# A fused transformer block on one core: how the first weights and tokens are loaded, and the order of the first microseconds

## The chip, the core and the metric

The kernel runs on one core of one Trainium2 chip. A core has a matmul engine (TensorE, PE in the profile, with its weight loads as PEld), VectorE (DVE), ScalarE (ACT), GpSimd (POOL) and SyncE (SP), which here only issues DMA transfers. Each engine works through its own list of instructions in order and waits on semaphores for the others. The metric is the device time of one execution in microseconds; lower is better.

## The reference

Input x is 2048 tokens of 448 values (D), in bf16. The block is an adaLN transformer layer:

```
mod = silu(c) @ w_mod                      # six rows of 448: sa, ca, ga, sb, cb, gb
h = layernorm(x) * (1 + ca) + sa
x = x + ga * A(h)                          # A: attention
h = layernorm(x) * (1 + cb) + sb
x = x + gb * B(h)                          # B: layernorm, 448->1792, gelu, 1792->448
```

A has 16 heads of 28 values. Each token sees 8 keys: itself and every second token before it, 14 back at the most. q, k and v come from one matrix wqkv (448 rows of 3 · 448).

## The kernel before

**Tiles.** Tokens are handled as even and odd streams (NS = 2), so that a window of 8 keys two apart becomes 8 neighbours in one stream. A tile p (0 to 7) holds 128 partitions with two tokens each: a row of x_all for one tile is two tokens of 448 bf16 values, 1792 bytes. The 448 input values of a matmul are three blocks of 128 rows and a rest of 64 rows; the rest rows are held twice, in the upper and the lower 64 partitions, so that two half-height matmuls can run for two outputs.

**The start.** Tile 0 and then tile 1 go through: statistics and normalization on VectorE (`stats` L455, `normalize` L477), transposes on TensorE into PSUM (`tr`, L532), scale and shift by the modulation into hT (`affine` L494), and the Q and K projections into qT and kT (`front_qk` L580). Tiles 2 to 7 go in pairs: their normalized rows are transposed by DMA (zT, L527), then `affine`, then the projection with the weights as moving operand (`natural_qk`, L614), whose result is again transposed by DMA into kT and qT (L631). Attention runs in 9 batches; the three matmuls of a batch's scores, sums and outputs are the lines L738, L760 and L771. V is made in L706 and L695, the output projection in L803, the two layers of B in L548 (through `summed`) and L883.

**The modulation.** c is turned into a column of PSUM by four matmuls (`c_cols`). silu is c / (1 + exp(−c)): exp on ScalarE, two operations on VectorE that leave the reciprocal in e_c, a product into silu_bf (128 × 4), and a ScalarE copy that repeats each of its columns 32 times into silu_bc. Then `mod_cols` makes the rows sa and ca as columns: matmuls over wm_st (three blocks of w_mod) and over wm_r (the rest).

**The staged weights of Q and K.** wqk_st holds three blocks of 128 rows with the Q and K columns of wqkv, wqr_st the 64 rest rows twice. In the projection of tiles 0 and 1 each head takes 32 columns of the array: `spread` (L432) copies from wqk_st into Wqk with a step of 28 columns and runs of 32, so that each head's run reaches four columns into the next head. The last head's run reaches four columns past the end of K, and this is why the loads take 900 columns instead of 896.

**Loads.** `load` (L317) puts transfers on SP's list. In the order of the list before: x tile 0, w_mod blocks, two halves of the w_mod rest, x tile 1, Q, K block 0, the two rest loads, blocks 1 and 2, x tiles 2 and 3 in one, x tiles 6 and 7, V's blocks, one V rest, x tiles 4 and 5, and so on.

**What sets the order.** Every step is a task, made by `add` with its engine, and the program order is a list written out by hand: ORDER names tasks by number, with a letter where a task goes to another than its first engine; SLOTS gives each buffer its place in its room (P is PSUM). `emit` walks through both. An entry such as `55+12@55` puts twelve filler matmuls over zeros ahead of task 55 on TensorE. The durations in the calls of `add` are estimates that are not used when the list is there. What an engine does next is thus fixed, and only semaphores decide when.

Of the kernel before, what the change touches and what calls it, by code (L numbers as in the profile page):

```python
# [49 lines left out]
]  # L50
ORDER = """
3 14 17 0 1 15 5 9 10 18 11 16 13 19 20 2 6 24 21 73 55+12@55 26 12 71 25 56 72 74 57 75 22 58 77 23 59 60 27 62 61 76
32 4 67 66 68+11@68 78 63 28 108 64 30 110 69 79 84:A 89:P 31 65 70 109 111 80 88:P 83 34 81 112:P 87:A 29 101+9@101
85 90:A 93:P 36 114 94+3@94 82 95 113 102 92:A 91 115:D 86 103 116 96 120:A 144 97 99 104 106 117:A 135 98 118:A 142
105 119:A 145 143 133 100 146 121 136 134 126 137 148 107 147 149:D 7 138 127 150 122 124 139 129 190 123 198 191 140
200 128 141 125 199 269 271 130 236 270 40 207 33 209 38 201 241 208 210 237 211 185 35 39 242 202 8 187 151:A 238 154
239 153 152 186 212 159 203 213 188 204 214:D 155 240 215 278 205 279 280 156 160 206 307:R 281 161 243 282 272 192
273:A 37 157 189 171 162 308:D 194 172 283 193 244 218 173 163 219 195 275 158 284 196 216 167 217 285 246 447:P 197
286 164 168 165 228 169:D 174 274 309 276:D 312 277 220 313 310 314 166 221 229 225 230 224 311 170 222:D 247 315 245
176 317 316 175 226 248 233 232 318 227 290 249 289:A 319 287:A 43 234 223 288 320 250 558:P 46 45 559 321 47 231 253  # L60
345 342 346 251 560 303 482:P 252 44 324 343 322 291 254 561 323 325 347 326 344 292 304 255 327 293 348 328 373:R 256
305 329 294 257 350 258 375 378 52 330 376 340:R 53 333 235 379 377 334 331 374 296 300 332 41 295 259 351 49 335 380
299 336 341 337 260 297 382 262 381 263 301 261 349 264 338:A 352 483 383 339 384 265 484 266 449 353 267 485 385 268
# [3 lines left out]
487 401 490 454 403 402 436 453 455 370 444 404 434 371:D 456 372 491 457 488 405 459 493 458 460 445 492 435 494 461  # L67
# [3 lines left out]
513 515:D 547 599 516 564 602 481 568 569 570 604 571 603 546 605 572 548 606 573 628 607 608 574 549 635 575 550 609  # L71
612 636 577 630 578 637 610 629 576 640 579 638 581 639 611 613 580 582 583 641 631 586 633 587 651 584 614 632 585
616 588 615 617 642 618 648 646 647 621 654 634 619 645 622 652 620 656 649 623 644 658 643 625 624 650 589 590 626
591:A 664 655 627 653 439 657 592 659 556 665 662 663 674 666 660 661 669 667 675 668 678 676 679 677 686 672 673 671
687 681 670 680 690 691 694 697 693 682 688 692 685 695 683 689 701 684 698 696 709 699 710 702 711 712 705 700 703
706 704 707 708
# [77 lines left out]
def kernel(  # L154
# [68 lines left out]
    silu_bf = cst.tile([128, KT], BF16, name="silu_bf")  # L223
# [739 lines left out]
```

## Time and profile before

| | |
|---|---|
| median of 3 runs | 168.64 us (167.93 to 169.38) |
| the profiled execution | 169.75 us, its span 168.1 us |
| busy | TensorE 96%, VectorE 69%, ScalarE 61%, GpSimd 28% |
| granted clock of TensorE | full, over the whole span |
| DMA | 18.78 MB in 35574 packets, mean 112 GB/s |

A line of the page or of an answer from the trace names engine, line of the kernel, operation, the tile written and the tiles read, the shape and the number of instructions. In a timeline the first two numbers are the start (microseconds from the start of the span) and the length; brackets give how long the engine was idle before it and which engine or transfer ended that. A letter q behind an engine (SPq) is its sequencer, which issues transfers. The span runs from the first to the last instruction; the execution's own time has 1.65 us beside it.

### The profile page before, as it was taken

Reading aid. Unit: us, or ns where it says so; the run is one execution under the profiler, and the core shown is the slowest. Engines: PE = TensorE matmul, PEld = TensorE weight load, DVE = VectorE, ACT = ScalarE, POOL = GpSimd, SP = SyncE. Lnnn points to the kernel's source line nnn. Section 1 sums busy time; section 2 is a strip of 40 time slices with the busy share of each in tenths; the row PEclk is TensorE's granted clock in tenths of the full one; section 3 lists DMA queues with packets and bytes.
Section 4 is the critical chain, followed back from the end, with each engine's and each line's share of the span. In section 5 each row is a group of like instructions: output and inputs, shape, how many; then the busy total and the mean of one; then the engine's idle time right before and its main releaser. Section 6 shows DMA issues by size and latency. Waiting matters only on the chain.

```text
span 168.1 us, 4962 instructions
## 1 busy us (share of the span) xinstructions
PE 161.5 (96%) x2126; PEld 83.4 (50%) x2126; DVE 115.8 (69%) x271; ACT 102.7 (61%) x142; POOL 47.7 (28%) x76
## 2 busy tenths in 40 slices
PE   7989989999997999999999999999999999999992
PEld 4768544345544544435565444556434455444562
DVE  6869899879899689998738877474798930400032
ACT  3368987779489954759866376956627730097300
POOL 4135252300361201269300113820003870007200
PEclk9999999999999999999999999999999999999999
DMA  5999989799997999910091000008110027110003
GB/s 153 325 335 297 168 265 134 152 201 170 221 200 182 236 150 236 169 35 0 4 139 46 4 0 0 4 0 97 35 55 0 0 43 195 49 60 0 0 0 109
DMA packets 35574, 18.78 MB, mean 112 GB/s; under 512 B 28508, under 2 KB 34593, under 8 KB 35553
## 3 DMA queue, kind: packets, MB, share of 16 engines
q1 hardware_dynamic: 35548, 18.47, 53.0%
q8 instruction: 16, 0.26, 0.7%
q14 instruction: 6, 0.04, 0.1%
q10 hardware_dynamic: 4, 0.00, 0.0%
HBM read 9.81 MB, written 1.84 MB: 69 GB/s over the span
## 4 chain that ended last, share of the span: by engine, by line
PE 81%; DMA 10%; DVE 2%; POOL 2%; issue 1%; SPq 1%; ACT 1%; POOLq 0%; DVEq 0%
PE p L883 26%; PE p L548 22%; PE pw L803 7%; PE pq L548 6%; PE p L554 4%; DMA x_all<-in_A_x_dram 4%; PE po L771 3%; PE lt L738 3%; PE pv L706 3%; PE pv L548 3%; DMA wm_st<-in_w_mod_dram 3%; DMA zT<-zy 2%; DMA kT<-zy 2%; PE pq L554 1%; PE pd L760 1%
## 5 line engine op out<-in xcount | busy, mean ns | idle before, releaser
L864 ACT ACTIVATE hm<-p,b_col 128x512 bf16<-128x512 f32 x56 | 33.9, 692 | 29.9 <-PE p L554 27.3
L883 PE MATMUL p<-w_s,hm 128*128 128x448 bf16 (+1 forms) x238 | 44.1, 342 | 0.0
L548 PE MATMUL p<-yT,w_s 128*128 128x512 bf16 x168 | 38.1, 379 | 0.0
L469 POOL TENSOR_TENSOR rs_all<-mvs,neg_half 128x2 f32<-128x2 f32 x22 | 16.7, 766 | 57.9 <-DVE mvs L458 57.8
L883 PEld LDWEIGHTS <-hm 128*128 128x128 bf16 x238 | 22.7, 98 | 19.2 <-issue 0.8
L889 DVE TENSOR_TENSOR x_all<-p,x1p 128x896 bf16<-128x896 f32 (+2 forms) x10 | 8.9, 902 | 25.9 <-PE p L883 25.9
L548 PEld LDWEIGHTS <-w_s 128*128 128x128 bf16 x168 | 15.8, 98 | 20.9 <-issue 2.9
L456 DVE BATCH_NORM_STATS2 stt<-x_all 128x6 f32<-128x448 bf16 x32 | 18.7, 610 | 1.2 <-DMA x_all<-in_A_x_dram 1.0
L745 ACT ACTIVATE et<-lt 128x928 bf16<-128x928 f32 x18 | 16.1, 947 | 5.3 <-PE lt L738 5.1
L841 POOL TENSOR_TENSOR x1p<-x_all,gbb_bc 128x448 f32<-128x448 bf16 x16 | 17.8, 1134 | 0.0
L548 PE MATMUL pq<-wqk_st,hT 128*128 128x448 bf16 x72 | 15.2, 354 | 0.6 <-DVE hT L502 0.5
L788 DVE TENSOR_TENSOR qT<-po,den 128x912 bf16<-128x912 f32 x9 | 9.9, 1104 | 7.0 <-ACT den L782 5.6
L751 DVE TENSOR_TENSOR et<-et,mask 128x928 bf16<-128x928 bf16 x18 | 11.6, 672 | 2.4 <-ACT et L745 2.4
L803 PE MATMUL pw<-wo_s,qT 128*128 128x448 bf16 x64 | 13.2, 353 | 0.0
L780 ACT ACTIVATE den<-pd 128x928 f32<-128x928 f32 x9 | 8.5, 940 | 5.8 <-PE pd L760 5.7
L819 DVE TENSOR_TENSOR h<-h,mod_bc 128x896 bf16<-128x896 bf16 x16 | 11.1, 709 | 0.3
L548 PEld LDWEIGHTS <-hT 128*128 128x128 bf16 x72 | 6.4, 98 | 7.7 <-issue 1.3
L628 ACT CAST zy<-pq 128x896 bf16<-128x896 f32 x10 | 9.0, 906 | 2.0 <-PE pq L554 1.9
L810 DVE TENSOR_TENSOR x_all<-pw,x_all 128x896 bf16<-128x896 f32 x8 | 8.7, 1088 | 1.7 <-PE pw L803 1.5
L782 ACT ACTIVATE den<-den,den_bias 128x928 f32<-128x928 f32 x9 | 9.6, 1072 | 0.2
L478 DVE TENSOR_SCALAR zy<-h,mvs,rs_all 128x448 bf16<-128x448 bf16 x16 | 6.6, 456 | 4.4 <-POOL rs_all L469 4.3
L456 DVE BATCH_NORM_STATS2 stt<-h 128x6 f32<-128x448 bf16 x16 | 9.4, 613 | 0.2
(115 smaller groups left out, 183.4 us busy)
## 6 DMA issues: line engine op xcount, KB each, us to landing
w_s<-in_B_w_dram SPq DMA_DIRECT2D x7, 224.0 KB, 4.2
out_dram<-x_all SPq DMA_DIRECT2D x7, 224.0 KB, 2.2
x_all<-in_A_x_dram SPq DMA_DIRECT2D x3, 448.0 KB, 6.0
wmod<-in_w_mod_dram SPq DMA_DIRECT2D x3, 448.0 KB, 7.0
w_s<-in_B_w_dram SPq DMA_DIRECT2D x3, 448.0 KB
wqk_st<-in_A_wqkv_dram SPq DMA_DIRECT2D x3, 225.0 KB
wm_st<-in_w_mod_dram SPq DMA_DIRECT2D x1, 672.0 KB
x_all<-in_A_x_dram SPq DMA_DIRECT2D x2, 224.0 KB, 2.6
```

The costliest lines, as they stand in the source:

```text
L456: add("DVE", 0.53, lambda: nc.vector.bn_stats(out=stt[:, w, b, 0:6], in_=src()), reads=reads, bufs=bufs, after=early if w == b == 0 else ( ...
L469: ways = {"POOL": (0.55 + 0.17 * n, lambda: nc.gpsimd.tensor_tensor(out=r, in0=v, in1=neg_half[:, 0:n], op=ALU.pow))}
L548: nc.tensor.matmul(out(), lhsT=lhs(kt, slice(0, 128)), rhs=rhs(kt, slice(0, 128)), start=first and kt == 0, stop=not first and kt == KT - 2)
L745: exps.append(add("ACT", 0.83, lambda half=half, lt=lt: nc.scalar.activation(out=et.t[:, 2 * half:2 * half + 2].rearrange("p r m c -> p r ...
L751: nc.vector.tensor_tensor(out=ev, in0=ev, in1=mask[:], op=ALU.mult)
L782: exps.append(add("ACT", 0.96, lambda: nc.scalar.activation(out=den.t[:], in_=den.t[:], func=ACT.Exp, scale=-1.0, bias=den_bias[:]), bufs= ...
L788: nc.vector.tensor_tensor(out=qT[:, :, LEAD + q00:LEAD + q00 + 2 * WQ], in0=po.t[:, :, 0:NS * 4 * WQ].rearrange("p j (m c) -> p m j c", c=WQ),
L803: nc.tensor.matmul(pw.t[:, s, 0:D], lhsT=qT[:, KT * s + ft, LEAD + 128 * p:LEAD + 128 * p + 128], rhs=wo_s[:, ft, :], start=(ft == 0), sto ...
L819: add("DVE", 0.55, lambda vec=vec, op=op: nc.vector.tensor_tensor(out=h2.t[:], in0=h2.t[:], in1=vec.unsqueeze(1).to_broadcast([128, NS, D] ...
L841: add("POOL", 1.0, lambda n=n: nc.gpsimd.tensor_tensor(out=x1p.t[:, n, :], in0=xn(p, n), in1=gbb2_bc[:], op=ALU.add), reads=[f"x{p}", "gbb ...
L864: gelus.append(add("ACT", 0.585, lambda f=f, a=a, p1=p1s[g]: nc.scalar.activation(out=hm.t[:, f].rearrange("p n c -> p (n c)"), in_=p1.t[: ...
L883: nc.tensor.matmul(p2.t[:, n, 0:c1 - c0], lhsT=hm.t[:, f, n, q * 128:(q + 1) * 128], rhs=w2_s[:, f, c0:c1], start=(f == parts[0][0]), stop ...
```

## The change

Five edits, all at the start of the program, with the order list and the buffer list made anew:

- wqk_st and wqr_st become 928 columns wide. The loads bring 896 columns, and two memsets on VectorE, beside that of neg_half, set the four columns behind them to zero. The copies of `spread` wait for them.
- The two halves of each rest (of w_mod, of Q and K, of V) come in one load of 128 partitions, whose source has a leading dimension of 2: step 0 where the same rows are wanted twice, step D for w_mod.
- x tiles 2 and 3 are two loads.
- silu's product and its repetition are one VectorE operation, which writes silu_bc from e_c, read with step 0, and PSUM. The ScalarE copy is gone, and so is silu_bf.
- The two memsets of one_cb move from between tile 0's two statistics to ahead of that operation.

Tasks are numbered anew (three fewer), so nearly every number in ORDER differs. With the numbers put back, each engine's list differs in these places only:

| engine | before | after |
|---|---|---|
| SP | ... x1, QK block 0, rest, rest, block 1, block 2, x2 and x3, x6 and x7, V, V rest, x4 and x5, ... | ... x1, QK block 0, block 1, rest, block 2, x2, x3, x6 and x7, V, x4 and x5, ... (V rest whole, behind the first block of the later w_mod load) |
| TensorE | 12 fillers, c, 11 fillers, modulation rest, blocks, last column; 9 fillers, projection of tile 0 (one piece), 3 fillers, four pieces, tile 1's transposes, the third Q piece, the half-row pieces, ... | 8 fillers, c, 10 fillers, modulation blocks, last column, rest; 9 fillers, five pieces, the third Q piece, the half-row pieces, tile 1's transposes, ... |
| VectorE | one copy of `spread`, tile 1's two normalizations, copy, tail, copy | three copies, two normalizations, tail |
| ScalarE | the silu_bc copy | gone |

The buffer list gives two of the first PSUM tiles each other's places and moves one zy tile; what follows is the old sharing with other numbers.

The diff without the two lists:

```diff
-    wqk_st = sb("hm", [128, KT - 1, 2 * D + HP - DH], BF16, "wqk_st")
-    wqr_st = sb("h2", [128, 2 * D + HP - DH], BF16, "wqr_st")
+    wqk_st = sb("hm", [128, KT - 1, 2 * D + HP], BF16, "wqk_st")
+    wqr_st = sb("h2", [128, 2 * D + HP], BF16, "wqr_st")
...
-    dconst(0.06, lambda: nc.vector.memset(neg_half[:], -0.5), ["neg_half"])
+    def make_half():
+        nc.vector.memset(neg_half[:], -0.5)
+        nc.vector.memset(wqk_st.t[:, :, 2 * D:2 * D + HP - DH], 0.0)
+        nc.vector.memset(wqr_st.t[:, 2 * D:2 * D + HP - DH], 0.0)
+
+    dconst(0.2, make_half, ["neg_half", "wqpad"], [wqk_st, wqr_st])
...
-        load(lambda: nc.sync.dma_start(out=wqk_st.t[:, kt, :], in_=A_wqkv[kt * 128:kt * 128 + 128, 0:2 * D + HP - DH]), 0.62, [f"wqk{kt}"],
+        load(lambda: nc.sync.dma_start(out=wqk_st.t[:, kt, 0:2 * D], in_=A_wqkv[kt * 128:kt * 128 + 128, 0:2 * D]), 0.62, [f"wqk{kt}"],
...
-    def load_rest(a):
-        load(lambda a=a: nc.sync.dma_start(out=wqr_st.t[KS * a:KS * a + KS, :], in_=A_wqkv[(KT - 1) * 128:D, 0:2 * D + HP - DH]),
-             0.5, [f"wr{a}"], bufs=[wqr_st])
+    def both(src, n):
+
+        return bass.AP(src.tensor, src.offset, [[n, 2], *src.ap])
+
+    def load_rest():
+        load(lambda: nc.sync.dma_start(out=wqr_st.t[:, 0:2 * D], in_=both(A_wqkv[(KT - 1) * 128:D, 0:2 * D], 0)),
+             0.5, ["wr0", "wr1"], bufs=[wqr_st])
...
-        for a in range(2):
-            load(lambda a=a: nc.sync.dma_start(out=Wv[KS * a:KS * a + KS, KT - 1, :], in_=A_wqkv[(KT - 1) * 128:D, 2 * D:3 * D]),
-                 0.2, [f"wvr{a}"])
+        load(lambda: nc.sync.dma_start(out=Wv[:, KT - 1, :], in_=both(A_wqkv[(KT - 1) * 128:D, 2 * D:3 * D], 0)), 0.3, ["wvr0", "wvr1"])
...
-    for v in range(2):
-        load(lambda v=v: nc.sync.dma_start(out=wm_r.t[KS * v:KS * v + KS, :], in_=w_mod[(KT - 1) * 128:D, v * D:v * D + D]),
-             0.25, [f"wmr{v}"], bufs=[wm_r])
+    load(lambda: nc.sync.dma_start(out=wm_r.t[:], in_=both(w_mod[(KT - 1) * 128:D, 0:D], D)), 0.4, ["wmr0", "wmr1"], bufs=[wm_r])
...
-    load_rest(0)
-    load_rest(1)
-    load_x(2, 4)
+    load_rest()
+    load_x(2, 3)
+    load_x(3, 4)
...
-    add("DVE", 0.08, lambda: nc.vector.tensor_tensor(out=silu_bf[:], in0=e_c[:], in1=psc.t[:, 0, 0:128 * KT:128], op=ALU.mult),
-        reads=["e_c"], bufs=[psc], writes=["silu"], name="silu")
-    add("ACT", 0.18, lambda: nc.scalar.copy(out=silu_bc[:], in_=silu_bf[:].unsqueeze(2).to_broadcast([128, KT, HP])),
-        reads=["silu"], writes=["silu_bc"], name="silu_bc")
+    add("DVE", 0.2, lambda: nc.vector.tensor_tensor(
+        out=silu_bc[:], in0=e_c[:].unsqueeze(2).to_broadcast([128, KT, HP]),
+        in1=psc.t[:, 0, :].rearrange("p (k n) -> p k n", n=128)[:, :, 0:HP], op=ALU.mult),
+        reads=["e_c"], bufs=[psc], writes=["silu_bc"], name="silu_bc")
```

More of the change, by code (lines that the diff above doesn't have):

```diff
@@ L43 @@
 SLOTS = [
[6 rows of a table removed]
[6 rows of a table added]
 ]
 ORDER = """
[L52 to L60, printed above, removed]
@@ L72 @@
[L72 to L76, printed above, removed]
+3 14 17 0 1 15 5 9 10 18 11 16 13 19 2 6 70 53+8@53 23 20 21 54 24 68 22 69 71 55 56 72 12 25 57 74 26 59 60+10@60 58
@@ new lines @@
+73 30 61 4 64 63 75 65 27 66 105 76 29 107 81:A 86:P 32 62 67 106 108 77 80 28 78 84:A 85:P 98+9@98 87:A 91 109:P 82
+88 92 34 79 83 99 90:P 89:A 100 111 93 110 94 96 112:D 101 141 103 113 132 95 117:A 139 102 114:A 142 140 130 115:A
+143 133 116:A 131 134 145 97 118 144 146:D 7 135 147 123 136 104 195 124 119 197 121 126 137 187 138 196 266 120 188
+268 125 267 122 204 38 233 206 31 127 198 36 205 207 208 33 238 234 37 199 182 8 239 148:A 151 184 235 150 149 236 209
+156 200 210 183 201 211:D 152 237 212 185 275 202 276 277 153 157 203 304:R 278 158 240 279 269 189 270:A 35 154 186
@@ new lines @@
+168 159 305:D 191 169 280 190 241 215 170 160 216 192 272 155 281 193 213 164 214 282 243 444:P 194 283 161 165 162
+225 166:D 171 271 306 273:D 309 274 217 310 307 311 163 218 226 222 227 221 308 167 219:D 244 312 242 173 314 313 172
+245 223 230 229 315 224 287 246 286:A 316 284:A 41 231 220 285 317 247 555:P 44 43 556 318 45 228 250 342 339 343 248
+557 300 479:P 249 42 321 340 319 288 558 251 320 322 344 323 341 289 301 252 324 290 345 325 370:R 253 302 326 291 254
+347 255 372 375 50 327 373 337:R 51 330 232 376 374 331 328 293 371 297 39 329 292 256 348 47 332 377 296 333 338 334
@@ new lines @@
+257 294 379 259 378 260 298 258 346 261 335:A 349 480 380 336 381 262 481 263 446 350 264 482 382 265 445 351 303 590
[3 rows of a table added]
+400 399 433 450 452 367 441 401 431 368:D 453 369 488 454 485 402 456 490 455 457 442 489 432 491 458 492 434 514 459
+435 493 591 460 494 461 533 495 463 534 522 464 536 462 498 592 465 521 535 499 496 593 466 497 500 501 502 515 503
+524 467 526 468 525 504 469 523 470 528 507 516 505 527 519 472 517 506 473 508 471 520 537 539 518 548 509 529 474
+532 541 530 550 531 476 511 554 475 562 597 477 559 540 563 549 598 538 594 560 551 564 595 542 552 510 512:D 544 596
@@ new lines @@
+513 561 599 478 565 566 567 601 568 600 543 602 569 545 603 570 625 604 605 571 546 632 572 547 606 609 633 574 627
+575 634 607 626 573 637 576 635 578 636 608 610 577 579 580 638 628 583 630 648 584 581 611 629 582 613 585 612 614
+639 615 645 643 644 618 651 631 616 642 619 649 617 653 646 620 641 655 640 622 621 647 586 587 623 588:A 661 652 624
+650 436 654 589 656 553 662 659 660 671 663 657 658 666 664 672 665 675 673 676 674 683 669 670 668 684 678 667 677
+687 688 691 694 690 679 685 689 682 692 680 686 698 681 695 693 706 696 707 699 708 709 702 697 700 703 701 704 705
@@ L222 @@
     e_c = cst.tile([128, KT], FP32, name="e_c")
-    silu_bf = cst.tile([128, KT], BF16, name="silu_bf")
     silu_bc = cst.tile([128, KT, HP], BF16, name="silu_bc")
@@ L244, with dconst @@
     early = []
-    def dconst(us, fn, writes):
-        early.append(add("DVE", us, fn, writes=writes, after=[one], name="const " + writes[0]))
+    def dconst(us, fn, writes, bufs=()):
+        early.append(add("DVE", us, fn, writes=writes, bufs=bufs, after=[one], name="const " + writes[0]))
     def const(us, fn, writes, reads=()):
@@ L317, in load @@
     def load(fn, us, writes, bufs=(), reads=(), fills=()):
-        queue.append(add("SP", 0.5, fn, reads=reads, writes=writes, bufs=bufs, fills=fills, after=queue[-1:] if len(queue) < 4 else queue[3:4], xfer=us,
+        queue.append(add("SP", 0.5, fn, reads=reads, writes=writes, bufs=bufs, fills=fills, after=queue[-1:] if len(queue) < 3 else queue[2:3], xfer=us,
                          name="load " + writes[0]))
@@ L438, in spread @@
             dst, src = (lambda k0=k0, n=n: Wqk[:, k0:k0 + n, half]), (lambda k0=k0, n=n: heads(wqk_st.t[:, k0:k0 + n, half * D:half * D + D], H))
-            add("DVE", 0.06 + 0.18 * n, lambda dst=dst, src=src: nc.vector.tensor_copy(out=dst(), in_=src()), reads=[f"wqk{k}" for k in ks],
+            add("DVE", 0.06 + 0.18 * n, lambda dst=dst, src=src: nc.vector.tensor_copy(out=dst(), in_=src()), reads=["wqpad"] + [f"wqk{k}" for k in ks],
                 bufs=[wqk_st], writes=[f"W{half}{k}" for k in ks], port=True, name="spread",
@@ L446, in spread @@
             src = lambda rows=rows, c0=c0: heads(wqr_st.t[rows, c0:c0 + D // 2], H // 2)
-            add("DVE", 0.22, lambda rows=rows, src=src: nc.vector.tensor_copy(out=Wqr[rows, half], in_=src()), reads=[f"wr{a}"],
+            add("DVE", 0.22, lambda rows=rows, src=src: nc.vector.tensor_copy(out=Wqr[rows, half], in_=src()), reads=["wqpad", f"wr{a}"],
                 bufs=[wqr_st], writes=[f"Wr{half}{a}"], port=True, name="spread r",
@@ L455, in stats @@
     def stats(src, w, b, reads, bufs=()):
-        add("DVE", 0.53, lambda: nc.vector.bn_stats(out=stt[:, w, b, 0:6], in_=src()), reads=reads, bufs=bufs, after=early if w == b == 0 else (),
+        add("DVE", 0.53, lambda: nc.vector.bn_stats(out=stt[:, w, b, 0:6], in_=src()), reads=reads, bufs=bufs,
             writes=[f"st{w}_{b}"], name="stats")
```

5 lines of the change are left out of this document (removed), and 21 rows, old and new, of tables (ORDER, SLOTS).

## Prediction

> **What bounds the kernel now.** I read the page first, then the chain of waits in order of time, then TensorE's own waits, and then the first 23 us engine by engine. The page, section 1 and the engine line of section 4:
>
> ```profile
> span 168.1 us, 4962 instructions
> ...
> PE 161.5 (96%) x2126; PEld 83.4 (50%) x2126; DVE 115.8 (69%) x271; ACT 102.7 (61%) x142; POOL 47.7 (28%) x76
> ...
> PE 81%; DMA 10%; DVE 2%; POOL 2%; issue 1%; SPq 1%; ACT 1%; POOLq 0%; DVEq 0%
> ```
>
> TensorE is busy 96% of the span and carries 81% of the chain, so the question is where it is not. The answer on what TensorE waited for has five lines:
>
> ```profile
> PE ps_c L382 <- DVE warm_w L242: 1.3, 1, 1.3
> PE lt L738 <- issue: 0.8, 1, 0.8
> PE pq L548 <- DVE hT L502: 0.5, 1, 0.5
> PE pq L562 <- DVE Wqk L439: 0.4, 1, 0.4
> PE lt L738 <- DMA kT<-zy: 0.4, 1, 0.4
> ```
>
> The first is the start of the program. The others are single gaps of 0.4 to 0.85 us. That is all that a change at the start can collect, apart from the filler matmuls of the first 10 us, which stand in TensorE's busy time without being work. The pieces of the chain (start, length, what) show which gap belongs to what:
>
> ```profile
> 1.26 4.57 DMA wm_st<-in_w_mod_dram
> ...
> 5.85 0.43 SPq L325
> ...
> 6.32 6.00 DMA x_all<-in_A_x_dram
> ...
> 12.34 1.68 DVE stt L456 x3
> ...
> 17.56 3.38 DMA zT<-zy
> ...
> 21.04 1.71 DVE hT L502 x3
> ...
> 22.79 2.25 PE pq L548 x11
> ...
> 33.71 0.70 PE lt L738 x62
> ...
> 51.05 0.85 issue
> ```
>
> So up to 22.79 us the end is set by one thread: the load of x tiles 2 and 3 (6.32 to 12.32), their statistics, their transposes through the DMA, their affine step on VectorE, and the Q projection of tiles 2 and 3, for which TensorE waits 0.54 us. After it TensorE runs almost without a pause. Busy time by stretch (columns: PE, PEld, DVE, ACT, POOL busy, clock, DMA share, GB/s):
>
> ```profile
> 3.50:5.50 2.00, 2.00 (x12) 1.09 (x11) 1.72 (x8) 0.50 (x3) 0.00 (x0) 1.00 1.05 391
> 6.00:8.50 2.50, 2.41 (x48) 1.89 (x47) 2.40 (x15) 0.92 (x2) 0.61 (x1) 1.00 1.02 293
> 9.50:11.50 2.00, 1.57 (x17) 1.19 (x15) 1.61 (x6) 1.33 (x3) 0.79 (x2) 1.00 0.97 341
> 13.97:22.25 8.28, 8.24 (x194) 5.17 (x192) 7.27 (x25) 7.31 (x9) 4.69 (x11) 1.00 0.92 215
> 22.79:165.08 142.29, 141.03 (x1814) 69.29 (x1814) 96.71 (x193) 87.78 (x119) 38.73 (x47) 1.00 0.49 89
> ```
>
> Two second threads matter. From 13.97 to 22.25 TensorE is busy 8.24 of 8.28 us: whatever lets this block start earlier or later moves its end by as much, and only the 0.54 us behind it hides a delay. And the DMA engines are full (share 0.97 to 1.05) from 3.5 us on, but not at one rate: 391 GB/s while 1792-byte rows of w_mod are moved, 293 while the 1800-byte Q, K rows are, 341 after them.
>
> **The change, part by part.** In the order list, after its numbers are shifted for the joined tasks, each engine's order differs only in the first 16 us or so; the buffer numbers are, but for the first few PSUM tiles and two zy tiles, a renaming. From tile 1's projection on (`front_qk`, L580) the program is the old one. So the sum is made at 22.79 us and carried from there.
>
> *Rows of 1792 instead of 1800 bytes.* The staged rows are 3·128 + 2·64 = 512, that is 922 KB. At 293 GB/s they take 3.15 us; at 341, as what follows them, 2.70; at 391, as w_mod's rows of just the new length, 2.36. The gain for everything queued behind is 0 to 0.79 us. I take 0.45 to 0.79, since the low rate coincides with these rows and both neighbours have rows of 1792 bytes; 0 stays as a bound, because I see only a coincidence of rate and rows. [...]
>
> *Tiles 2 and 3 in two loads.* They do not help by themselves: VectorE's list begins these statistics with a half of tile 3 before and after the change, so it waits for the later load. Its place in the queue has the same bytes ahead. The third Q, K issue stands at 5.85, directly behind w_mod's landing (1.26 + 4.57 = 5.83); with fewer transfers ahead I expect tile 3's load to be the one that waits there, 0.47 us before the 6.32 of today's joined load. With the DMA engines full that is worth nothing. Net: tile 3 lands 0.45 to 0.79 us earlier, at 11.5 to 11.9.
>
> *What stands between it and TensorE.* VectorE must be free when it lands:
>
> ```profile
> 9.93 0.86 DVE L478 TENSOR_SCALAR zy<-x_all,mvs,rs_all 128x448 bf16<-128x448 bf16 x2 [0.18 <-POOL rs_all L469]
> 10.71 0.28 DVE L439 COPY Wqk<-wqk_st 128x512 bf16<-128x512 bf16 x1
> 10.91 0.18 DVE L491 COPY zy<-zy 128x128 bf16<-128x128 bf16 x1
> 11.02 0.28 DVE L439 COPY Wqk<-wqk_st 128x512 bf16<-128x512 bf16 x1
> ```
>
> It has finished by 11.30 today; the same operations are only reordered (both copies ahead of the two normalizations), so it is free at about 11.3 or before. The thread from 12.34 to 22.75 (statistics, GpSimd, transposes, affine) is unchanged and moves as one. Alone this would put tile 2's projection at 22.0 to 22.3.
>
> *The silu columns.* The two steps between e_c and silu_bc today:
>
> ```profile
> 5.38 0.20 ACT L467 ACTIVATE rs_all<-rs_all 128x2 f32<-128x2 f32 x1
> 6.19 0.30 ACT L398 COPY silu_bc<-silu_bf 128x128 bf16<-128x128 bf16 x1 [0.61 <-DVE silu_bf L396]
> ...
> 5.69 0.40 DVE L478 TENSOR_SCALAR zy<-x_all,mvs,rs_all 128x448 bf16<-128x448 bf16 x1 [0.33 <-ACT rs_all L467]
> 6.00 0.15 DVE L396 TENSOR_TENSOR silu_bf<-e_c,ps_c 128x4 bf16<-128x4 f32 x1
> 6.07 0.25 DVE L418 COPY wm_d<-wm_st 128x384 bf16<-128x384 bf16 x1
> ```
>
> The joined operation writes 128 values to each partition: above the 0.15 us for 4, below the 0.40 for 448, so about 0.25. It falls into the 0.33 us that VectorE idles before the normalization at 5.69. silu_bc would then be there by some 5.7 instead of 6.49. w_mod lands at 5.83, so the modulation matmuls could start 0.6 us earlier, but VectorE, which needs their result only after its statistics of tile 1, does not pass that on. What VectorE does gain is the 0.15 us of the removed operation's place and a little from the one_cb memsets that go into the idle time: 0.15 to 0.2 us for the affine steps of tile 0.
> *The added memsets and the joined rest loads.* One row for each:
>
> ```profile
> 1.28 0.06 DVE L270 MEMSET neg_half<- 128x4 f32 x1
> ...
> 1.73 1.20 SPq L349 DMA_DIRECT2D wm_r<-in_w_mod_dram  x2
> ```
>
> Two memsets of that size, 0.12 us, end within the wait for tile 0's rows. Three joins take three issues of 0.6 us off SP, one of them far behind, and the split adds one; with the DMA engines full that is zero, and if the engines ran dry it would bring the later transfers forward by up to 0.6 us. Eight fewer fillers are not work.
>
> *Tile 1's transposes behind tile 0's projection.* This costs. TensorE's list today and ScalarE's beside it:
>
> ```profile
> 11.05 0.39 PE L562 MATMUL pq<-hT,Wqk 128*128 128x256 bf16 x2 [0.43 <-DVE Wqk L439]
> 11.28 0.61 PE L535 MATMUL ptr<-ident,zy 128*128 128x128 bf16 x8
> 11.72 0.38 PE L562 MATMUL pq<-hT,Wqk 128*128 128x256 bf16 x2
> 12.04 0.61 PE L554 MATMUL pq<-hT,Wqr 64*128 64x256 bf16 x8
> ...
> 9.98 0.56 ACT L504 ACTIVATE hT<-ptr,mod_col 128x256 bf16<-128x256 bf16 x1
> 10.44 0.39 ACT L449 COPY Wqr<-wqr_st 64x256 bf16<-64x256 bf16 x1
> 11.93 0.57 ACT L504 ACTIVATE hT<-ptr,mod_col 128x256 bf16<-128x256 bf16 x1 [1.10 <-PE ptr L535]
> ```
>
> The pair at 11.05 no longer waits for a copy (it comes before the normalizations) but for ScalarE's affine step, which ends at 10.54, less 0.17: TensorE starts at 10.4. Then 0.23 for the pair, 0.32 for the next pair and the switch to half rows, 0.54 for the eight half-row matmuls: the transposes start at about 11.5, 0.2 us later than today. ScalarE's four affine steps of tile 1 follow at 12.1 to 14.05. The block at 13.97 has 0.11 us to spare against them (1.93 us of steps from 11.93), so it starts 0.1 us late and ends at 22.35.
>
> *Sum.* The projection of tiles 2 and 3 starts at the later of 22.35 (TensorE) and 22.0 to 22.3 (its data): 22.35 instead of 22.79, a gain of 0.44 us. Behind it ScalarE, SP and VectorE hang on the same two threads, so I carry it whole; the gap before the scores at 33.7 us (0.4) and the one that waited for "issue" at 51.05 (0.85) I leave. The profiled execution took 169.75 us, 168.1 of span and 1.65 around it; it would be 169.3. The median of the runs is 1.11 us lower, so 168.64 − 0.44 = **168.2 us**.
>
> **Rivals.** First, *the rows are not slower for their length*: the 293 GB/s is a disturbance of the memory, and tile 3 lands at 12.3 as today. For it: 341 GB/s afterwards is not 391 either, with rows of 1792 bytes. Then the projection starts at 22.79 as before, TensorE idles where the fillers were, and the time is 168.6. [...]
>
> Second, on the other side, *VectorE stuck behind the third weight transfer*. Its two copies of the third row block now stand ahead of tile 1's normalizations. If that block lands after 10.4 us, the copies, 0.78 us of normalizations and the 0.18 us copy end after 11.9, the transposes start 0.65 us late, and the block behind reaches 22.79 too late; landing at 10.7, the latest today's copy allows, gives 23.2, so 0.4 us slower: 169.0. Against it: both earlier blocks and the half rows go ahead as today, and any gain in rate brings it forward.
>
> Third, *more than the sum*: the later gaps (0.4 at 33.7, 0.85 at 51.05) do not come again with other timing, and tile 1 is not held up: 0.44 + 0.1 + 0.4 + 0.85 = 1.8 us, 166.8. For it: neither gap is a steady cost of a repeated instruction; against it: nothing there is changed.
>
> **How the numbers follow.** Forecast 0.5, first rival 0.27, second 0.12, third 0.11. The runs of the kernel before spread by 0.7 us to either side, so 1% (1.7 us) is about what can be told from no change. The range runs from the third rival to the second with part of that spread on top: 166.8 to 169.4. Forecast and first rival are "within 1%" whole, the second nearly, the third by half: faster 0.08, same 0.86, slower 0.06.
>
> **What would show it.** Right: over 340 GB/s between 6 and 8.5 us; VectorE's statistics of tile 3 at 11.5 to 11.9; the transposes of tile 1 behind the half-row matmuls at about 11.5 and a new TensorE gap of about 0.7 us before 14; no gap at 22.3. Wrong: DMA at 293 GB/s and statistics at 12.3 (first rival); the copies of Wqk waiting for the DMA past 10.4 (second). The sum is also wrong if the projection does start earlier and the scores at 33.7 wait longer for kT by the same amount. A TensorE that stays on its slower pace beyond 9 us, having fewer fillers, would show as longer matmuls in the first projection.

## The result, and the profile after

The changed kernel is slower, where no measurable change was forecast: 176.67 us median of 6 runs (175.95 to 177.89) against 169.02 us of the kernel before beside it (6 runs, 167.93 to 169.68). The ratio is 1.046, with an interval of 1.041 to 1.051. That is 7.6 us; the forecast was 168.2 us, with a range up to 169.4. The profiled execution took 176.53 us, 174.8 of it span, against 169.75 and 168.1. Here and below, medians and ranges hold all runs, and ratios leave out the few that lie over 1.5% above the fastest of their kernel.

The page of the changed kernel: span, busy time, the granted clock in 40 slices, the chain's shares.

```profile
span 174.8 us, 4947 instructions
...
PE 163.4 (93%) x2118; PEld 84.3 (48%) x2118; DVE 116.1 (66%) x273; ACT 102.3 (59%) x141; POOL 47.1 (27%) x76
...
PEclk9968799999999999999999999999999999999999
...
PE 81%; DMA 9%; ACT 3%; DVE 2%; SPq 2%; issue 1%; DVEq 0%
```

TensorE is busy about as long as before (163.4 us against 161.5), in a span that is 6.7 us longer: it stands still more. And its clock, full over the whole span before, now dips in slices 3 to 5, which are 8.7 to 21.9 us. What TensorE waited for (in all, times, longest, in us):

```profile
PE pq L565 <- ACT Wqk L444: 3.6, 1, 3.6
PE ps_col L413 <- DMA wm_r<-in_w_mod_dram: 1.5, 1, 1.5
PE ps_c L385 <- DVE warm_w L240: 1.3, 1, 1.3
...
```

The first two lines are new, and both lead to joined rest loads: wm_r itself, and a copy (L444) that stands on ScalarE behind a copy of the rest of Q and K. The chain shows this in a row (start, length, what):

```profile
3.88 11.68 DMA wqr_st<-in_A_wqkv_dram
...
15.58 0.40 ACT Wqr L452
15.98 0.53 ACT Wqk L444
...
16.56 1.47 PE pq L565 x6
18.03 0.97 PE pq L557 x8
19.00 0.80 PE ptr L538 x8
...
19.82 1.94 ACT hT L507 x4
```

One load of 229 KB needs 11.68 us to land, while the DMA engines move more than that in each microsecond. The stretches show what happens meanwhile, first after, then before (busy PE, PEld, DVE, ACT, POOL, granted clock, DMA share, GB/s):

```profile
10.00:15.00 5.00, 2.96 (x15) 1.87 (x13) 1.05 (x6) 0.56 (x1) 0.00 (x0) 0.74 0.99 278
15.00:20.00 5.00, 3.44 (x26) 2.17 (x27) 3.46 (x11) 1.86 (x5) 1.61 (x3) 0.66 0.44 141
```

```profile
10.00:15.00 5.00, 4.57 (x49) 3.54 (x48) 3.94 (x13) 3.90 (x9) 0.95 (x2) 1.00 1.05 372
15.00:20.00 5.00, 5.00 (x110) 3.14 (x109) 4.83 (x15) 4.11 (x5) 2.14 (x8) 1.00 0.88 168
```

All engines run dry between 10 and 15 us; DMA alone stays busy, at 278 instead of 372 GB/s. The clock of 0.74 and 0.66 is a mean: in shorter stretches it is half behind each of the two waits, and nearly full between them.

```profile
9.40:11.00 1.60, 1.21 (x6) 0.84 (x6) 1.50 (x8) 0.89 (x2) 0.43 (x1) 0.50 0.96 302
...
12.90:16.50 3.60, 0.06 (x1) 0.00 (x0) 0.51 (x2) 0.92 (x3) 0.74 (x2) 0.94 0.81 256
16.50:18.00 1.50, 1.44 (x8) 0.73 (x10) 0.95 (x3) 0.76 (x3) 0.87 (x2) 0.50 0.13 49
```

TensorE's timeline after, from the end of its wait to the Q projection of tiles 2 and 3 (L551, the last line but one) and the piece behind that (L557):

```profile
16.56 1.47 PE L565 MATMUL pq<-hT,Wqk 128*128 128x256 bf16 x6 [3.60 <-ACT Wqk L444]
17.96 1.04 PE L557 MATMUL pq<-hT,Wqr 64*128 64x256 bf16 x8
18.93 0.86 PE L538 MATMUL ptr<-ident,zy 128*128 128x128 bf16 x8
...
29.63 2.44 PE L551 MATMUL pq<-wqk_st,hT 128*128 128x448 bf16 x12
32.01 0.55 PE L557 MATMUL pq<-wqr_st,hT 64*128 64x448 bf16 x4
```

Before, one matmul of this projection ran early and the other eleven from 22.79 us, so the start of the piece behind it is the fair comparison:

```profile
21.89 0.36 PE L548 MATMUL pq<-wqk_st,hT 128*128 128x448 bf16 x1
...
24.98 0.55 PE L554 MATMUL pq<-wqr_st,hT 64*128 64x448 bf16 x4
```

32.01 − 24.98 = 7.03 us, and the span is 6.7 us longer: the whole loss lies ahead of this point.

Why one load lags is seen in the trace's completion events. An ordinary load here has sixteen completion reports, as many as the page counts DMA engines. (The two loads of c, one row each, have two, before and after.) These are the times of all reports, in us, of some loads of the changed kernel (a pair far behind the rest is set apart):

```
load                      issued   reports
rest of w_mod, joined     1.72     2.80 |                     7.84  8.05
x tile 1                           fourteen, 5.88 to  6.75 |  8.39  8.49
Q, K block 0                       fourteen, 6.58 to  7.47 |  9.01  9.08
Q, K block 1                       fourteen, 7.25 to  8.04 |  9.56  9.66
rest of Q, K, joined      3.88     4.87 |                    15.31 15.55
Q, K block 2              4.48     fourteen, 8.11 to  8.77 | 15.86 15.88
x tile 2                           fourteen, 8.80 to  9.33 | 16.41 16.47
x tile 3                           fourteen, 9.48 to 10.28 | 16.99 17.01
```

A joined load has one report 1.0 us after its issue and then only two late ones; the others have sixteen. In the kernel before, each half rest has sixteen, from 7.43 to 9.05 us. From the two late reports I infer that a joined load is carried by two engines, 64 rows each. Those two then fall behind in everything that follows: fourteen sixteenths of x tile 3 were there at 10.28 us, before the 12.3 of the old kernel, and two sixteenths came at 17.0. VectorE's last copies out of block 2 waited for all sixteen: they began at 15.91, behind the report at 15.88. Why it is two, no run shows. In the trace's record of the issues, each of these joined loads has destination sizes of 1 and 128, and each half in the kernel before 64 and 1.

### The profile page after: what moved, and what is told of

Its sections match the earlier page's. It is cut to its first block, busy times and chain, and to the rows that moved or that the text cites. A ratio compares the mean times of both kernels' runs of the same rounds, so it can differ in the third digit from the quotient of the medians.

```text
span 174.8 us, 4947 instructions
## 1 busy us (share of the span) xinstructions
PE 163.4 (93%) x2118; PEld 84.3 (48%) x2118; DVE 116.1 (66%) x273; ACT 102.3 (59%) x141; POOL 47.1 (27%) x76
## 4 chain that ended last, share of the span: by engine, by line
PE 81%; DMA 9%; ACT 3%; DVE 2%; SPq 2%; issue 1%; DVEq 0%
PE p L886 25%; PE p L551 21%; PE pw L806 7%; DMA wqr_st<-in_A_wqkv_dram 7%; PE pq L551 6%; PE p L557 4%; PE pv L709 4%; PE lt L741 3%; PE po L774 3%; DMA zT<-zy 3%; PE pv L551 3%; PE pq L557 2%; PE pd L763 1%; ACT hT L507 1%; PE pq L565 1%
## 5 line engine op out<-in xcount | busy, mean ns | idle before, releaser
L551 PE MATMUL p<-yT,w_s 128*128 128x512 bf16 x168 | 38.1, 379 | 0.0
L551 PEld LDWEIGHTS <-w_s 128*128 128x128 bf16 x168 | 15.9, 98 | 20.9 <-issue 2.9
L551 PE MATMUL pq<-wqk_st,hT 128*128 128x448 bf16 x72 | 15.0, 353 | 0.1
L551 PEld LDWEIGHTS <-hT 128*128 128x128 bf16 x72 | 6.5, 98 | 7.0 <-issue 1.2
```

Of the source, the lines that this page charges most:

```text
L551: nc.tensor.matmul(out(), lhsT=lhs(kt, slice(0, 128)), rhs=rhs(kt, slice(0, 128)), start=first and kt == 0, stop=not first and kt == KT - 2)
```

## The experiments

Two theories stood at the outset: the leading dimension of 2 puts a load on two engines, against the length of the single load, the order of the queue, or another of the five edits. Times are medians, with the kernel before timed beside each kernel; a ratio's interval is 95%. Four kernels were run once (the Q, K join alone, the two patterns without a join, the other source). A single time stands against the spread of the kernel before, 167.9 to 170.8 us in 23 runs, so it carries a conclusion only where the difference is well over that.

**The joins undone.** The changed kernel, with its order and all its other edits, but each joined load issued as two (shown for Q and K; V and w_mod likewise):

```diff
+    def halves(dst, src):
+        for a in range(2):
+            nc.sync.dma_start(out=dst(a), in_=src(a))
...
-        load(lambda: nc.sync.dma_start(out=wqr_st.t[:, 0:2 * D], in_=both(A_wqkv[(KT - 1) * 128:D, 0:2 * D], 0)),
+        load(lambda: halves(lambda a: wqr_st.t[KS * a:KS * a + KS, 0:2 * D], lambda a: A_wqkv[(KT - 1) * 128:D, 0:2 * D]),
```

> The changed kernel with its three joined loads (rest of w_mod, of Q and K, of V) each issued as two loads of 64 partitions again; order lists, row length, tiles 2 and 3 apart and the silu operation as changed. Theory (two engines): a load whose source has a leading dimension of 2 is carried out by two of the sixteen DMA engines, and these two then hold up a sixteenth share each of every later load. Then all of the loss is in the joins: the rest of Q and K lands by about 9 us instead of 15.6, and the time goes from 176.7 to within 1% of the kernel before, 168 to 169.5. Rival (order): the loss comes from the new order (rests behind block 1, transposes of tile 1 behind the half-row matmuls) or from fewer fillers and the lower clock they leave: then it stays above 174.

Measured: 169.36 us (12 runs, 168.28 to 171.87) against 168.96; ratio 1.003 (0.9995 to 1.006). The whole loss is in the joins; the rest of the change moves the time by no more than the interval, which holds 1. That is the same measured result as the forecast for the whole change, but not by its sum, as the next section shows.

**One join alone, Q and K.** The kernel before, with only this load joined:

```diff
-        load(lambda a=a: nc.sync.dma_start(out=wqr_st.t[KS * a:KS * a + KS, :], in_=A_wqkv[(KT - 1) * 128:D, 0:2 * D + HP - DH]),
...
+            src = A_wqkv[(KT - 1) * 128:D, 0:2 * D + HP - DH]
+            if a:
+                nc.sync.dma_start(out=wqr_st.t[:], in_=bass.AP(src.tensor, src.offset, [[0, 2], *src.ap]))
```

> The kernel before with one edit: the two rest loads of Q and K are one load of 128 partitions whose source has a leading dimension of 2 with step 0. Theory (two engines): each of two engines gets 64 rows of 75 to 100 ns, 5 to 6 us more work than today, so the rest lands at 12 to 14 us instead of 8.7, the later weight and token loads land 4 to 6 us late, and the time is 172 to 175. Rival (order): no order is changed, so 168 to 169.5.

Measured: 173.69 us (one run) against 168.96, so about 4.7 us, inside the 172 to 175 of the theory. (The 75 to 100 ns of a row there are packet times in the trace of before: the middle half of its 512 packets of 1800 bytes took 75 to 100 ns.) The load needed 9.19 us to land, and its copy stood on GpSimd, with the half-row part of tile 0's projection behind it (GpSimd's timeline):

```profile
13.38 0.40 POOL L455 COPY Wqr<-wqr_st 64x256 bf16<-64x256 bf16 x1 [5.54 <-DMA wqr_st<-in_A_wqkv_dram]
```

**One join alone, w_mod.** Likewise, with a step of 448 (D) instead of 0:

```diff
+                nc.sync.dma_start(out=wm_r.t[:], in_=bass.AP(src.tensor, src.offset, [[D, 2], *src.ap]))
```

> The kernel before with one edit: the two halves of the w_mod rest come in one load with a leading dimension of 2 (step 448 values, no row read twice). Theory (two engines): 64 rows of 41 ns on each of two engines, 2.3 us more than its share of 8 rows; it lands at about 8 us instead of 6.2, the modulation and everything that the two engines carry later is late by about as much, and the time is 170 to 171.5. Rival (only re-reading the same rows, step 0, is slow): 168.5 to 169.5.

Measured: 170.59 us (4 runs, 170.26 to 171.54) against 168.25; ratio 1.014 (1.009 to 1.020), so 2.3 us. What TensorE waited for, and a stretch of its windows:

```profile
PE ps_col L415 <- DMA wm_r<-in_w_mod_dram: 2.6, 1, 2.6
```

```profile
9.50:11.50 2.00, 2.00 (x36) 1.80 (x33) 1.79 (x7) 0.94 (x2) 1.01 (x2) 0.50 0.92 263
```

TensorE waits 2.6 us, until the load lands at about 9.1 (8 was expected), with two late reports, 8.70 and 9.09 us, and right behind that runs at half its clock. Step 0 is not needed for the loss: 448 does it too. (The 41 ns of a row in the theory are the median of the 896-byte packets in the trace of before.)

**One join alone, V.** The kernel of the first experiment, with V's rest joined as in the change:

```diff
-        load(lambda: halves(lambda a: Wv[KS * a:KS * a + KS, KT - 1, :], lambda a: A_wqkv[(KT - 1) * 128:D, 2 * D:3 * D]), 0.3, ["wvr0", "wvr1"])
+        load(lambda: nc.sync.dma_start(out=Wv[:, KT - 1, :], in_=both(A_wqkv[(KT - 1) * 128:D, 2 * D:3 * D], 0)), 0.3, ["wvr0", "wvr1"])
```

> The changed kernel with the joined loads of the w_mod rest and of the Q, K rest undone and that of the V rest kept. Theory (two engines): it lands some 2.3 us later and delays a sixteenth of each transfer behind it on two engines, but V's first matmuls come at 18 us and the later weights are wanted after 26 us, so no cost: 168.5 to 169.8. If it does cost, above 170.5.

Measured: 169.74 us (10 runs, 168.48 to 172.75); ratio to the kernel before 1.003 (0.999 to 1.007), as without this join. So a two-engine load that nobody wants soon costs nothing that these runs can tell. The two that are wanted soon add up to 4.7 + 2.3 = 7.0 of the 7.6 us, where the 4.7 comes from a single run. Engines can also fall behind without a join: in this kernel's profile, fourteen reports of w_mod's blocks had come by 5.75 us and two came at 7.04 and 7.07, long before V's rest was issued at 10.82. Why is open.

**The leading dimension, without a join.** Joining changes three things at once: the pattern, the size of the load and the number of issues. So two kernels keep both half loads at their size and place and change the pattern alone. The first reads its 64 rows as 2 times 32 neighbouring rows:

```diff
-        load(lambda a=a: nc.sync.dma_start(out=wqr_st.t[KS * a:KS * a + KS, :], in_=A_wqkv[(KT - 1) * 128:D, 0:2 * D + HP - DH]),
...
+            (pitch, n), cols = src.ap
+            nc.sync.dma_start(out=wqr_st.t[KS * a:KS * a + KS, :], in_=bass.AP(src.tensor, src.offset, [[pitch * n // 2, 2], [pitch, n // 2], cols]))
```

> The kernel before with one edit: its two rest loads of Q and K stay two loads of 64 partitions with the same rows and bytes, but the source is written with a leading dimension of 2 (2 times 32 rows). Theory (two engines, set by the leading dimension): both loads go to the same two engines, 64 rows each, so the delays are those of the joined load: rest at 12 to 14 us, 172 to 175 in all. Rival (joining itself: one transfer over 128 partitions that reads each row twice is slow): nothing is joined, so 168 to 169.5.

Measured: 169.42 us (one run), and sixteen reports for each load (7.36 to 8.26 and 7.72 to 8.83 us). The theory missed here. But the two dimensions join without a seam into one of 64 rows, and so can be read as one. That this happens is inferred from the sixteen reports; the trace's record of the issue bears it out, with destination sizes of 64 and 1 as in the kernel before, where the next kernel has 1 and 64. The second cannot be read so: even rows, then odd ones:

```diff
+            nc.sync.dma_start(out=wqr_st.t[KS * a:KS * a + KS, :], in_=bass.AP(src.tensor, src.offset, [[pitch, 2], [2 * pitch, n // 2], cols]))
```

> The kernel before with one edit: the two rest loads of Q and K stay two loads of 64 partitions with the same bytes, but the source runs first over the even and then over the odd rows, a leading dimension of 2 that cannot be folded with the next one (in the earlier run with 2 times 32 neighbouring rows it could be, and all sixteen engines took part). The rest rows land permuted, so Q and K are not the reference's. Theory (two engines, by the leading dimension alone): each of the two engines gets 32 rows of each load, 64 in all, as in the joined load; the rest lands at 12 to 14 us and the time is 172 to 175. Rival (the joining: 128 partitions in one transfer, or each row read twice): nothing is joined, 168 to 169.5.

Measured: 175.68 us (one run) against 168.25, 0.7 us above the range of the theory. The late reports are two for each load, 10.66 and 11.44 us for the first, 13.88 and 14.63 for the second. Start of the chain's part, and the copy that waited:

```profile
5.34 9.70 DMA wqk_st<-in_A_wqkv_dram
15.04 0.02 issue
15.06 0.30 DVE Wqk L444
```

```profile
11.56 0.40 POOL L455 COPY Wqr<-wqr_st 64x256 bf16<-64x256 bf16 x1 [3.92 <-DMA wqr_st<-in_A_wqkv_dram]
```

No join, no step 0, no larger load, no other order, and 7.4 us lost: the leading dimension alone does it. The chain now runs through wqk_st, an ordinary load right behind the two (9.70 us to its landing), which by the same inference the two engines hold up.

**How much of the loss is the clock.** After the wait for Q and K, the changed kernel's TensorE runs on half its clock (0.50 from 16.5 to 18 us). Fifteen more of the kernel's own filler matmuls (256 columns, adding zeros to a sum that is in use) are meant to keep the clock up; that they do was the author's assumption. Where they stand is written in the order list (so many fillers ahead of a task, into the sum of another), and `filler` now adds to that sum instead of starting one. In the first of two kernels they stand one piece too late, behind the piece that waits:

```diff
-88 92 34 79 83 99 90:P 89:A 100 111 93 110 94 96 112:D 101 141 103 113 132 95 117:A 139 102 114:A 142 140 130 115:A
+88 92 34 79 83 99 90:P 89:A 100+15@91 111 93 110 94 96 112:D 101 141 103 113 132 95 117:A 139 102 114:A 142 140 130 115:A
...
-            nc.tensor.matmul(t.sums[0].t[:, 0, 0:256], lhsT=warm_w[:, 0:128], rhs=warm_w[:, 0:256], start=True, stop=True)
+            nc.tensor.matmul(t.sums[0].t[:, 0, 0:256], lhsT=warm_w[:, 0:128], rhs=warm_w[:, 0:256], start=n != 15, stop=n != 15)
```

> The changed kernel with one edit: 15 more filler matmuls (256 columns of zeros, added to an open sum) ahead of the projection piece for which TensorE waits 3.6 us, so that it does not stand still there. The late rest load is untouched. If the lower granted clock of 10 to 20 us is a second part of the loss: the 3.24 us that the pieces from 16.6 to 19.8 take fall to about 1.7, and the time goes from 176.7 to about 175.2. If the clock costs nothing beside the late load: 176.7.

Measured: 178.3 us, ratio 1.060 (1.052 to 1.068). TensorE's timeline shows the fillers behind the wait, as work that delays:

```profile
16.75 0.61 PE L565 MATMUL pq<-hT,Wqk 128*128 128x256 bf16 x2 [3.35 <-ACT Wqk L444]
17.14 3.41 PE L385 MATMUL pq<-warm_w 128*128 128x256 bf16 x15
```

They put over 3 us on the path and cost 1.6 us by the medians (178.3 − 176.67), 2.4 us by the ratios (1.060 and 1.046, each to runs of the kernel before beside it). This kernel does not test what it was made for. But its profile has a wait of 3.35 us with a granted clock of 1.00 from 10 to 20 us, and TensorE is slow there all the same: the fifteen fillers behind the wait take 227 ns each, where nine take 1.14 us, 127 ns each, at 8.28 us in the kernel before. So a clock given as 1.00 does not rule out a slow stretch.

In the second kernel they stand ahead of that piece (with the same second edit):

```diff
-88 92 34 79 83 99 90:P 89:A 100 111 93 110 94 96 112:D 101 141 103 113 132 95 117:A 139 102 114:A 142 140 130 115:A
+88 92 34 79 83 99+15@91 90:P 89:A 100 111 93 110 94 96 112:D 101 141 103 113 132 95 117:A 139 102 114:A 142 140 130 115:A
```

> The changed kernel with 15 more filler matmuls, this time ahead of the very piece for which TensorE waits 3.6 us (in the run before they stood one piece too late, behind the wait, and lengthened the path). The late rest load is untouched. If the lower granted clock is a second part of the loss: TensorE is at full clock from 16.6 us on, the 3.24 us of pieces up to 19.8 fall to about 1.7, and the time is about 175.2 instead of 176.7. If the clock costs nothing beside the late load: 176.7.

Measured: 175.4 us (4 runs, 175.33 to 176.84), ratio 1.038 (1.033 to 1.044).

```profile
15.03 2.42 PE L385 MATMUL pq<-warm_w 128*128 128x256 bf16 x15
18.56 1.06 PE L565 MATMUL pq<-hT,Wqk 128*128 128x256 bf16 x6 [1.11 <-ACT Wqk L444]
19.55 0.61 PE L557 MATMUL pq<-hT,Wqr 64*128 64x256 bf16 x8
20.09 0.62 PE L538 MATMUL ptr<-ident,zy 128*128 128x128 bf16 x8
```

The granted clock is now 1.00 from 10 to 20 us, and the eight-matmul and six-matmul groups take 0.61 and 1.06 us instead of 1.04 and 1.47. From the first of them to the end of the transposes it is 2.15 us instead of 3.23 (18.93 + 0.86 − 16.56): in this stretch of the two profiles the lower clock costs 1.1 us. That it is a part of the loss in time is not shown. By the medians the fillers gain 1.3 us, but the two intervals overlap. The mean granted clock, recorded with each of the changed kernel's six executions, does not show it either: the two at 1.00 took 176.44 and 176.81 us, the two at 0.98 took 176.53 and 175.95. But under the same 1.00 nine fillers at 11.88 us, ahead of this stretch, take 2.08 us, 231 ns each: a recorded 1.00 does not rule out slow stretches, and this settles little.

In this profile the late load itself ended 2.0 us later than in the changed kernel's (17.56 instead of 15.55). One engine was behind already with w_mod's blocks, which are issued ahead of any joined load: fifteen reports had come by 5.47 us, the last at 7.65. The landing of such a load is thus not the same in each execution. The granted clock was 0.50 behind the changed kernel's two waits, and 1.00 both with these fillers and behind the wait of 3.35 us above.

**The rows alone.** The kernel before, with loads of 896 columns (shown for a block; the rest likewise) and the two memsets of the change:

```diff
-        load(lambda: nc.sync.dma_start(out=wqk_st.t[:, kt, :], in_=A_wqkv[kt * 128:kt * 128 + 128, 0:2 * D + HP - DH]), 0.62, [f"wqk{kt}"],
+        load(lambda: nc.sync.dma_start(out=wqk_st.t[:, kt, 0:2 * D], in_=A_wqkv[kt * 128:kt * 128 + 128, 0:2 * D]), 0.62, [f"wqk{kt}"],
```

> The kernel before with one edit: rows of Q and K loaded as 896 columns with the memsets of the four columns behind them. By the prediction's step: 340 to 390 GB/s instead of 293 between 6 and 8.5 us, tile 3 lands 0.45 to 0.79 us earlier than 12.3, the 0.54 us gap of the matmul engine at 22.3 goes, and the time falls by 0.4 to 0.55 us (0.997 of before). Rival (the rate was a disturbance, 8 bytes cost nothing): 293 GB/s stays, no change.

Measured: 168.95 us (12 runs); ratio 1.002 (0.998 to 1.006). The stretch in which these rows are moved:

```profile
6.00:8.50 2.50, 2.50 (x46) 1.86 (x45) 2.40 (x15) 0.92 (x2) 0.61 (x1) 1.00 1.05 277
```

277 GB/s, against 293 with the longer rows: the low rate does not come from the eight bytes. Yet in this profile tile 3 landed at 11.62 us instead of 12.32, and the gap of 0.54 us is gone, both as expected. The rows need not be the reason: with the same short rows the next kernel's profile has it at 12.52, and with the long ones a kernel above (2 times 32 rows) at 11.98. The landing is the last of sixteen reports, and in the kernel before fifteen had come by 11.45.

**Where the low rate is from.** The same kernel, its three Q, K blocks read out of w_mod:

```diff
-        load(lambda: nc.sync.dma_start(out=wqk_st.t[:, kt, 0:2 * D], in_=A_wqkv[kt * 128:kt * 128 + 128, 0:2 * D]), 0.62, [f"wqk{kt}"],
+        load(lambda: nc.sync.dma_start(out=wqk_st.t[:, kt, 0:2 * D], in_=w_mod[kt * 128:kt * 128 + 128, 2 * D:4 * D]), 0.62, [f"wqk{kt}"],
```

> The kernel with only the shorter rows (896 columns, memsets behind them), and its three 128-row loads of Q and K read the same number of rows and bytes out of w_mod instead of wqkv, so that Q and K are not the reference's. It asks where the low rate between 6 and 8.5 us comes from. If it is the source (rows 2688 bytes apart, of which every second starts off a multiple of 256 bytes): 340 GB/s or more there instead of 277. If it is the moment (what else happens at 6 to 8.5 us): 270 to 300 again.

Measured: 318 GB/s in that stretch, and 169.3 us (one run). The array that is read was to give 340 or more, the moment alone 270 to 300; 318 is neither. That it matters where a row starts was the author's guess, and this run does not show it. Where the low rate comes from stays open.

**What is left of the change, in the old order.** The kernel before with the shorter rows, tiles 2 and 3 in two loads and the joined silu operation, all rests in halves:

```diff
+        step = 1 if p0 == 2 else p1 - p0
+        load(lambda: [nc.sync.dma_start(out=x_all[:, p:p + step, :], in_=xv[:, p:p + step, :]) for p in range(p0, p1, step)], 0.63 * (p1 - p0),
...
+    add("DVE", 0.2, lambda: nc.vector.tensor_tensor(
+        out=silu_bc[:], in0=e_c[:].unsqueeze(2).to_broadcast([128, KT, HP]),
+        in1=psc.t[:, 0, :].rearrange("p (k n) -> p k n", n=128)[:, :, 0:HP], op=ALU.mult),
```

> The order, the buffers and the split rest loads of the kernel before, with three parts of the change: rows of 896 columns, tiles 2 and 3 in two loads, silu in one VectorE operation. Without the joined loads and the new order, tile 3 should land at 11 to 11.7 us, the projection of tiles 2 and 3 start at 22.2 instead of 22.8, and the time be 0.3 to 0.6 us below that of the kernel before (0.997). Rival (such gains are taken back at the later gaps, as in the kernel with only the joins undone): no difference within 0.3%.

Measured: 168.59 us (12 runs, 167.81 to 169.93) against 169.1; ratio 0.997 (0.994 to 0.9999). It has the lowest median here, by 0.3%, with an interval that ends just below 1; among this many comparisons that is a possible gain and not a shown one. Its profile has tile 3's statistics and the projection of tiles 2 and 3 here:

```profile
11.81 1.68 DVE L463 BATCH_NORM_STATS2 stt<-x_all 128x6 f32<-128x448 bf16 x3 [0.73 <-DMA x_all<-in_A_x_dram]
```

```profile
21.71 2.51 PE L555 MATMUL pq<-wqk_st,hT 128*128 128x448 bf16 x12
24.16 0.55 PE L561 MATMUL pq<-wqr_st,hT 64*128 64x448 bf16 x4
```

The piece behind the projection starts 0.82 us earlier than before (24.16 instead of 24.98), and the time is 0.5 us less. These events are early in the experiment on the rows too (statistics at 11.65, that piece at 24.05 in its profile), whose time did not move. One profile of an early start is no gain in time.

## Why the prediction was wrong

**The step that failed.** Under *The added memsets and the joined rest loads* the prediction valued the joins at zero "with the DMA engines full", with up to 0.6 us as a gain and nothing on the side of a loss. It priced the issues on SP and took the transfer for the same bytes over the same sixteen engines. That was not read anywhere: no load of the kernel before has a leading dimension of 2, so its trace could not show the price (the loads of c, with two reports instead of sixteen, were the one sign in it that a load need not use all engines), and the step should have had a bound above zero. One follows from its own rows. Had it asked which engines carry the load, two engines with 115 KB each, at a sixteenth of 391 GB/s, need 4.7 us by themselves, an estimate, and with their shares of the other loads more; 11.68 was measured for the load. With the Q, K rest and w_mod's rest measured at 4.7 and 2.3 us apart, V's at nothing, and everything else at nothing, 7.0 of the 7.6 us are accounted for. In the changed kernel the two stand one behind the other on the same two engines, with their last reports at 8.05 and 15.55. The remaining 0.6 us I have not placed: the single joins were measured in the old order, and one of them once.

**The closing sentence on TensorE's pace** named the slower pace, but for another reason. (In the trace of before, the first twelve fillers take 2.74 us, 228 ns each, and the nine at 8.28 us 127 ns each.) It comes with the joins here, not with fewer fillers: in the changed kernel the nine fillers at 9.79 us take 2.08 us, 231 ns each, at a granted clock of 0.50; with the joins undone and the same few fillers they take 1.14 us (at 8.11), the granted clock is 1.00 over the whole span and the time is that of before. In the profile the lower clock lengthens one stretch by 1.1 us; as a part of the loss in time it is not shown.

**The rows.** The prediction took 0.45 to 0.79 us for them. Alone they moved the time by a ratio of 1.002 (0.998 to 1.006), and the rate stayed at 277 GB/s. So the first rival was right about the row's length. A coincidence of rate and rows was taken for a cause. That tile 3 did land 0.70 us earlier in that profile, inside the forecast, is no evidence for it: the landing moves by as much from one profile to another.

**The sum, with the joins undone.** Then the rest of the working can be held against a trace. Chain of the kernel of the first experiment:

```profile
5.06 4.54 DMA wqr_st<-in_A_wqkv_dram
...
9.72 0.41 POOL Wqr L457
...
10.20 0.85 POOL rs_all L476
...
11.08 0.87 DVE zy L485 x2
...
12.00 0.63 PE ptr L542 x8
```

- *The projection of tiles 2 and 3* starts at 22.44, with all twelve matmuls in a row. The forecast's 22.35 was for the last eleven, so it does not compare with this start. The piece behind the projection starts here, 0.17 us earlier than the 24.98 of before, where 0.44 was forecast; and the path to it is another:

```profile
24.81 0.55 PE L561 MATMUL pq<-wqr_st,hT 64*128 64x448 bf16 x4
```

- *Tile 1's transposes* were put at 11.5 and start at 12.00. Not TensorE's order decides but GpSimd: its share of tile 1's statistics (rs_all) stands behind its copy of the rest, which now lands at 9.60 since block 1 is issued ahead of it. The prediction looked at the copies on VectorE and not at the load that was moved past another, though SP's new order stands first in the table of the change.
- *No gain shows in the time.* The medians of this kernel and of the kernel before say +0.4 us, their two profiled executions −0.8 (168.97 and 169.75), so a gain of 0.17 us can't be followed. The two later gaps that the prediction left in place (0.4 at 33.7, 0.85 at 51.05) are not there as they were; the profile has these two waits instead:

```profile
PE lt L745 <- DVE zy L498: 0.5, 1, 0.5
PE po L778 <- issue: 0.4, 1, 0.4
```

**Right** were the small ones. VectorE's timeline in the changed kernel's trace, and then the affine step of tile 0 in that of the first experiment:

```profile
5.31 0.29 DVE L399 TENSOR_TENSOR silu_bc<-e_c,ps_c 128x128 bf16<-128x128 f32 x1
5.52 0.39 DVE L481 TENSOR_SCALAR zy<-x_all,mvs,rs_all 128x448 bf16<-128x448 bf16 x1
...
15.91 0.51 DVE L442 COPY Wqk<-wqk_st 128x512 bf16<-128x512 bf16 x2 [4.86 <-DMA wqk_st<-in_A_wqkv_dram]
```

```profile
8.44 0.73 DVE L509 TENSOR_SCALAR hT<-ptr,mod_col 128x256 bf16<-128x256 bf16 x2
```

The joined silu operation takes 0.29 us (0.25 forecast) and stands in VectorE's idle time; the normalization behind it starts at 5.52 instead of 5.69. With the joins undone, tile 0's affine step starts at 8.44 instead of 8.60, 0.16 us earlier (0.15 to 0.2 forecast). The second rival, VectorE stuck behind the third block, happened in a form that it did not mean: its last two copies of Wqk waited 4.86 us, for the two engines' shares of that block.

## What to carry to other kernels

Two loads joined into one by a leading dimension of 2 were not the same transfer with an issue less: here the join cost 4.7 us with Q and K's rest and 2.3 with w_mod's. So before such an edit, look at the outermost dimension of the pattern, and after it count the load's completion reports, which here were two late ones instead of sixteen. Price it by the bytes for each engine that seems to carry it, at each engine's rate (115 KB at a sixteenth of 391 GB/s, 4.7 us, an estimate below the 11.68 measured), and remember that the loads behind it wait for the same slow engines: fourteen shares of block 2 were there by 8.77 us and the last at 15.88. When the trace of before has no row for a kind of transfer, its cost has a bound on both sides, and zero is not one because the engines are full.

## What the runs showed of the hardware

- Loads whose source led with a dimension of 2 had two late completion reports instead of sixteen: with step 0, with step 448, and with even rows ahead of odd ones. The joined rest of Q and K (229 KB, step 0) needed 9.2 to 13.5 us in four profiles, where two halves needed 4.5 (with the joins undone).
- A source of 2 times 32 neighbouring rows, where the two dimensions continue each other, did not do this: sixteen reports for each load (7.36 to 8.26 and 7.72 to 8.83 us).
- The lag carries over: fourteen shares of block 2 by 8.77 us and two at 15.86 and 15.88. The profile's DMA share is 0.99 from 10 to 15 us all the same, so a full share is no sign that sixteen engines are at work for the load that matters.
- The joined load of V's rest, issued at 10.82 us and complete at 19.5, cost nothing measurable (1.003, 0.999 to 1.007).
- The granted clock of TensorE was 0.50 in stretches right behind waits of 1.5 to 5.2 us (9.4 to 11 and 16.5 to 18 us in the changed kernel, 9.5 to 11.5 with the joined w_mod rest, 15 to 20 with the even and odd rows). Behind a wait of 3.35 us in another profile it was 1.00, and fifteen fillers took 227 ns each even so.
- One or two engines were 1.3 to 2.2 us late with a load of sixteen shares and no join ahead of it (w_mod's blocks in two profiles); the reason is not known.
